# Chunk 1's softmax with tokens on partitions, a shorter weight conversion, and an identity made by VectorE

## The chip, the cores and the metric

The kernel runs on one core of one Trainium2 chip. The metric is the device time of one execution in microseconds (us). Before the change the median of three runs was 972.17 us (971.12 to 972.57).

## The reference

Pooled attention feeds a two-layer feed-forward net. Keys and values are averaged over groups of 8 positions, so each head of a batch has 72 pooled keys for 576 queries.

```python
def _attn_ref(q, k, v):                      # (8, 8, 576, 64) float32 each
    k_p = k.reshape(B, H, Sp, pool, D).mean(axis=3)
    v_p = v.reshape(B, H, Sp, pool, D).mean(axis=3)
    scores = scale * np.matmul(q, k_p.transpose(0, 1, 3, 2))
    scores = scores - np.max(scores, axis=-1, keepdims=True)
    attn = np.exp(scores)
    attn = attn / (np.sum(attn, axis=-1, keepdims=True) + 1e-09)
    return np.matmul(attn, v_p).astype(np.float32)

def _moe_ref(x, w_in, w_out):                # x (4608, 512); weights 512x2048 and 2048x512
    h = np.maximum(x @ w_in, 0.0)
    return (h * h @ w_out).astype(np.float32)
```

The two weight matrices arrive as 64-bit floats and are turned into 32-bit floats on the chip.

## The kernel before

**Chunks and steps.** The 4608 tokens are cut into 12 chunks of 384. Each chunk needs 16 steps, one for each 128 columns of the hidden layer. A step `(c, fc)` puts on TensorE the hidden product `h` of this step (line 480), then the pieces of attention that are due, then the output product `o` of two steps earlier (`project`, line 517, `LAG` = 2). ScalarE applies the ReLU and, in chunks 0 and 1, the square (`r`, lines 498 to 500). `h` has two PSUM buffers, so a new `h` waits until ScalarE has read the one before the last. Chunk 0 multiplies plain float32 (weights `wf`). Later chunks split every operand in a high and a low float32r part (`xh`, `xl`, `gh`, `gl`, `w`) and add three products.

**Attention.** It runs by pairs of heads, four pairs to a chunk: `transpose_q` (PSUM `qps`, copied to `st`), scores (`sps`), softmax, `weigh_values` (`av`, copied to `x`). Chunk 0 keeps tokens on partitions: `token_scores` (line 403) leaves 96 tokens by 4x72 keys, so that VectorE takes maxima and sums along the free axis (`tm`); `token_turn` (line 437) then turns the result with eight transposes (`pps`) and ScalarE copies it to `sc`. Chunk 1 and later keep the keys on partitions: `scores` (line 315) hands its copy to GpSimd, which reduces over partitions (`mx` for the maxima, `tot` for the sums), and the sums go through DRAM and back to become reciprocals (`rs`, `rc`, `rr`, `rd`, `rb`, lines 372 to 399).

**Weights.** Each of the 32 weight tiles (`raw`) is landed by a DMA. `magnitude` (ScalarE, one instruction) writes the absolute value of the high word to `wf`. `to_float32` (VectorE) then clips it, shifts and masks it, and ors in the sign bits and the top bits of the low word: four instructions, two keys at a time.

**What sets the order.** `InOrder` records each instruction in the order in which the program issues it, engine by engine, and an engine works it off in that order. Loads go out on SP's queue, in the order in which `load` was called before `issue_loads` (line 106). Before the steps comes a start that is written out by hand (lines 546 to 609): loads, pooling of batch 0's and batch 1's keys and values (chunk 1 holds tokens of both batches), and chunk 0's attention. Values are pooled on TensorE against a matrix of `ones` (`pool_v_pair`, PSUM `vps`). `keep_busy` multiplies the identity with itself. After that, a table `work` lists what is due at which step; `EARLY` gives the first step of each pair of chunk 1 and the offsets of its stages. The loop at the end (lines 653 to 674) reads it: first `h`, then what TensorE owes, then `project`, then the work of the other engines, the conversion, the loads, and ScalarE's `r` last.

```python
IDLE = (3, 1)
EARLY = ((-19, -16, -13, -10), (0, 2, 3, 5, 5, 6, 7, 8))
FIRST, EAGER, AHEAD = 2, 8, 5
```

PSUM pools: `ps_o` three banks (outputs, and chunk 0's scores), `ps_h` two, `ps_a` three (everything else).

Of the kernel before, what the change touches and what calls it, by code (L numbers as in the profile page):

```python
# [32 lines left out]
def pooled_attn_relu2_ffn(  # L33
# [281 lines left out]
    def scores(c, p):  # L315
# [3 lines left out]
        early = c == 1  # L319
        if early:  # L320

            blocks = st.rearrange("p (i t s) -> p i t s", i=2, s=QT)
            for i in range(2):
                h = 2 * p + i
                for t, (b, _, _) in enumerate(segments(c)):
                    for two in range(2):
                        rows = slice(two * D, (two + 1) * D)
                        PE.matmul(ss[two][:SP_, (i * 2 + t) * QT:(i * 2 + t + 1) * QT], lhsT=kf[b][rows, h // KH, h % KH * SP_:(h % KH + 1) * SP_],
                                  rhs=blocks[rows, i, t, :], start=True, stop=True)
        else:  # L330
            for i in range(2):
                h = 2 * p + i
                for b, o, n in segments(c):
                    kh, kl, _ = kv[b]
                    for j, kk in enumerate((kl, kh)):
                        PE.matmul(ss[i][:SP_, o:o + n], lhsT=kk[:, h * SP_:(h + 1) * SP_], rhs=st[:, i, o:o + n], start=j == 0, stop=j == 1)

        def then():
            if early:
                sc = w_tile(F32, f"sc_{c}_{p}")[:SP_, :, :CH]  # L340
                cols = sc.rearrange("p i (t s two) -> p two i t s", two=2, s=QT)
                for two in range(2):
                    ACT.copy(cols[:, two], ss[two][:SP_, :CH].rearrange("p (i t s) -> p i t s", i=2, s=QT))
            else:
                sc = sb.tile([SP_, 2, CH], F32, name=f"sc_{c}_{p}", tag="sc", bufs=SCB)
# [9 lines left out]
    def reduced(kind, c, p):  # L355
        names = [f"{kind}_{c}_{p}_{i}" for i in range(2)]
        if c == 1:
            return [half_tile("m", x)[:SP_, :CH] for x in names]
        return [sb.tile([SP_, CH], F32, name=x, tag="mx", bufs=3) for x in names]
# [345 lines left out]
```

## Time and profile before

| what | value |
|---|---|
| median of 3 runs | 972.17 us (971.12 to 972.57) |
| the profiled execution | 971.68 us, of which the span of its instructions 969.9 us |
| TensorE busy | 946.1 us, 98% |
| VectorE / ScalarE / GpSimd busy | 628.5 / 428.3 / 394.1 us |
| DMA | 64.45 MB, 66 GB/s over the span |

A line of the timeline gives start, duration, engine, operation, the tile written and the tiles read, shapes and the number of merged instructions; in brackets stands the idle time of the engine before it and what ended it. PEld is TensorE's weight load, SPq a DMA issued by SP. A float32 product with 128 or 96 columns shows as two records for each instruction, a transpose as one. Half tiles share a name: two keys, or two small tiles, show under the name of the first of them, so `wf_o` and `wf_i` both stand for converted weights of either matrix.

### The profile page before, as it was taken

How to read it: one execution, taken by the hardware profiler on the slowest of the kernel's cores; microseconds unless marked ns; L12 is line 12 of the kernel's file. 1: busy time of each engine (PE TensorE's matmuls, PEld its weight loads, DVE VectorE, ACT ScalarE, POOL GpSimd, SP SyncE). 2: the span in 40 equal slices, each digit the busy share in tenths (PEclk: the TensorE clock that was granted, in tenths of full speed). 3: DMA queues.
4: the chain of work that ended last, by engine and by line, in shares of the span. 5: the costliest groups of instructions: out<-in, count | busy, mean ns of one | idle time of the engine just before them, and what ended most of it. 6: DMA issues, size and time to landing. Idle time of an engine off the chain costs nothing.

```text
span 969.9 us, 13344 instructions
## 1 busy us (share of the span) xinstructions
PE 946.1 (98%) x4888; PEld 793.5 (82%) x4888; DVE 628.5 (65%) x1034; ACT 428.3 (44%) x847; POOL 394.1 (41%) x209
## 2 busy tenths in 40 slices
PE   5989899999999999999999999999999999999998
PEld 5644457888888888888888888888888888888997
DVE  4869997877765556767775656667776555453221
ACT  1644466774434445344444434443543434432322
POOL 4288733544344443443434335343534534440000
PEclk9999999999999999999999999999999999999999
DMA  9926212112211112112112102102311210100000
GB/s 239 365 95 217 82 34 66 48 52 87 60 45 62 38 38 70 34 51 92 54 39 76 37 20 78 52 30 52 95 52 30 77 32 18 58 10 9 33 1 32
DMA packets 53361, 64.45 MB, mean 66 GB/s; under 512 B 14936, under 2 KB 34480, under 8 KB 53296
## 3 DMA queue, kind: packets, MB, share of 16 engines
q1 hardware_dynamic: 53296, 63.61, 21.4%
q8 instruction: 38, 0.62, 0.3%
q14 instruction: 27, 0.22, 0.1%
HBM read 53.87 MB, written 9.71 MB: 66 GB/s over the span
## 4 chain that ended last, share of the span: by engine, by line
PE 85%; DVE 8%; issue 3%; DMA 2%; ACT 1%; POOL 0%; SPq 0%; DVEq 0%; POOLq 0%
PE o L29 38%; PE h L29 37%; PE av L29 4%; PE sps L29 3%; DVE wf_o L29 2%; DVE wf_i L29 2%; PE qps L29 1%; PE vps L29 1%; DMA q<-in_q_dram 1%; DMA rd<-rr 0%; DVE st L29 0%; PE kps L29 0%; DVE sc L29 0%; DVE kp L29 0%; POOL tot L29 0%
## 5 line engine op out<-in xcount | busy, mean ns | idle before, releaser
L29 PE MATMUL h<-xh,w_i 128*128 128x384 f32 x1408 | 389.1, 337 | 0.0
L29 POOL PARTITION_ALL_REDUCE tot<-sc x88 | 250.1, 2889 | 217.8 <-issue 201.6
L29 PE MATMUL o<-w_o,gh 128*128 128x512 f32 x1056 | 335.2, 398 | 0.4 <-ACT ob L29 0.4
L29 PEld LDWEIGHTS h<-xh,w_i 128*128 128x128 f32 x1408 | 258.7, 188 | 8.5 <-issue 0.5
L29 PE MATMUL h<-xl,w_i 128*128 128x384 f32 x704 | 238.0, 338 | 0.0
L29 PEld LDWEIGHTS o<-w_o,gh 128*128 128x128 f32 x1056 | 192.6, 188 | 52.1 <-issue 15.3
L29 POOL PARTITION_ALL_REDUCE mx<-sc x88 | 131.4, 1540 | 243.6 <-ACT sc L29 243.6
L29 DVE TENSOR_TENSOR gl<-r,gh 128x384 fp32r<-128x384 f32 x176 | 146.5, 832 | 108.4 <-ACT gh L29 106.5
L29 PE MATMUL o<-w_o,gl 128*128 128x512 f32 x528 | 208.7, 395 | 0.0
L29 DVE TENSOR_TENSOR r<-r 128x384 f32<-128x384 f32 x160 | 105.7, 661 | 108.7 <-ACT r L29 108.3
L29 ACT CAST gh<-r 128x384 fp32r<-128x384 f32 x176 | 90.4, 514 | 150.1 <-DVE r L29 149.6
L29 PEld LDWEIGHTS h<-xl,w_i 128*128 128x128 f32 x704 | 132.2, 188 | 8.1 <-issue 0.7
L29 ACT ACTIVATE r<-h 128x384 f32<-128x384 f32 x192 | 93.8, 488 | 99.9 <-PE h L29 98.6
L29 PEld LDWEIGHTS o<-w_o,gl 128*128 128x128 f32 x528 | 99.1, 188 | 22.5
L29 DVE TENSOR_TENSOR st<-qps,st 64x384 fp32r<-64x384 f32 x80 | 60.3, 754 | 48.1 <-ACT st L29 47.2
L29 ACT CAST st<-qps 64x384 fp32r<-64x384 f32 x80 | 59.4, 742 | 52.6 <-PE qps L29 52.0
L29 ACT ACTIVATE sc<-sc 72x384 f32<-72x384 f32 x88 | 43.7, 525 | 70.1 <-DVE sc L29 70.1
L29 ACT CAST xh<-rb 128x384 fp32r<-128x384 f32 x44 | 22.6, 513 | 108.5 <-DVE rb L29 108.5
L29 DVE TENSOR_REDUCE vp<-v 72x64 f32<-72x512 f32 x48 | 51.0, 1063 | 0.0
L29 DVE TENSOR_REDUCE kp<-k 96x64 f32<-96x512 f32 x42 | 43.7, 1041 | 3.4 <-DMA k<-in_k_dram 3.4
L29 DVE TENSOR_TENSOR sc<-sc,mx 72x384 f32<-72x384 f32 x88 | 44.6, 546 | 0.0
L29 PE MATMUL av<-sc,vp 72*64 72x384 f32 (+1 forms) x256 | 43.1, 425 | 0.9 <-ACT sc L29 0.9
(82 smaller groups left out, 701.8 us busy)
## 6 DMA issues: line engine op xcount, KB each, us to landing
k<-in_k_dram SPq DMA_DIRECT2D x48, 192.0 KB
out_dram<-ob SPq DMA_DIRECT2D x36, 256.0 KB
rb<-rd SPq DMA_DIRECT2D x88, 96.0 KB
raw_i<-in_moe_w_in_dram SPq DMA_DIRECT2D x16, 512.0 KB
raw_o<-in_moe_w_out_dram SPq DMA_DIRECT2D x16, 512.0 KB
v<-in_v_dram SPq DMA_DIRECT2D x48, 144.0 KB
q<-in_q_dram SPq DMA_DIRECT2D x30, 192.0 KB
q<-in_q_dram SPq DMA_DIRECT2D x32, 96.0 KB
```

What stands on the lines that cost most here:

```text
L29: return lambda *a, **k: self.tc.keep_in_program_order(f(*a, **k))
```

## The change

- The identity, which GpSimd made, is now made by VectorE (a ramp of indices, a transpose, four comparisons). `keep_busy` issues 16 and 2 products, not 3 and 1.
- `magnitude` scales the absolute value by 2^16, and a second ScalarE instruction writes the wanted top bits of the low word, as a whole number, over that word. `to_float32` then needs three VectorE instructions and not four.
- Chunk 1 uses `token_scores`, `token_normalise` and `token_turn` as chunk 0 does. Its exponentials read PSUM and take the negated maximum as bias, one instruction for each block of 72 keys. Its sums no longer go through DRAM, and GpSimd's reductions begin with chunk 2. `EARLY` has five stages and its first pair starts at step 0.
- Chunk 1's first query tile and two further weight tiles are loaded ahead of batch 1's values. Two of the four poolings of these values, and the transposes of batch 1's keys, move from the start into steps 0, 2 and 3. The copy of `vps` goes from VectorE to ScalarE.

```diff
-EXP_MIN = 2.0 ** -15
-EXP_MAX = 122879.9921875
+SHIFT = 2.0 ** 16
+EXP_MIN = 2.0 ** -15 * SHIFT
+EXP_MAX = 122879.9921875 * SHIFT
+LOW = 7.4999 / 65535
...
-    IDLE = (3, 1)
+    IDLE = (16, 2)
-    EARLY = ((-19, -16, -13, -10), (0, 2, 3, 5, 5, 6, 7, 8))
+    EARLY = ((-16, -13, -10, -7), (0, 1, 2, 3, 4))
...
-    make_identity(nc, ident)
+    ramp = const.tile([P, 2, 32], F32, name="ramp")
+    DVE.memset(ident, 0.0)
+    DVE.memset(ramp[:, 0, :1], 0.0)
+    for n in (1, 2, 4, 8, 16):
+        DVE.tensor_scalar(ramp[:, 0, n:2 * n], ramp[:, 0, :n], float(n), None, op0=ALU.add)
+    DVE.transpose(ramp[:, 1, :], ramp[:, 0, :])
+    for n in range(0, P, 32):
+        rows = slice(n, n + 32)
+        DVE.tensor_scalar(ident[rows, rows], ramp[rows, 0, :], ramp[rows, 1, :1], None, op0=ALU.is_equal)
...
-        ACT.activation(wf[key].rearrange("p (a n) -> p a n", a=2), words[..., 1].bitcast(F32), AF.Abs)
+        ACT.activation(wf[key].rearrange("p (a n) -> p a n", a=2), words[..., 1].bitcast(F32), AF.Abs, scale=SHIFT)
+        halves = raw[key].bitcast(U16).rearrange("p a (n w) -> p a n w", w=4)
+        ACT.activation(words[..., 0], halves[..., 1], AF.Copy, scale=LOW)
...
             DVE.tensor_scalar(m, m, EXP_MIN, EXP_MAX, op0=ALU.max, op1=ALU.min)
-        for _, _, m in parts:
-            DVE.tensor_scalar(m, m, 3, 0x3FFFFFF8, op0=ALU.logical_shift_left, op1=ALU.bitwise_and)
         for words, _, m in parts:
-            DVE.scalar_tensor_tensor(m, words[..., 1], 0xC0000000, m, op0=ALU.bitwise_and, op1=ALU.bitwise_or)
+            DVE.scalar_tensor_tensor(m, m, 3, words[..., 0], op0=ALU.logical_shift_left, op1=ALU.bitwise_or)
         for words, _, m in parts:
-            DVE.scalar_tensor_tensor(m, words[..., 0], 29, m, op0=ALU.logical_shift_right, op1=ALU.bitwise_or)
+            DVE.scalar_tensor_tensor(m, words[..., 1], 0x80000000, m, op0=ALU.bitwise_and, op1=ALU.bitwise_or)
...
-            DVE.tensor_copy(kv[b][2][:, 2 * p:2 * p + 2, :].rearrange("s h d -> s (h d)"), pt[:SP_, :2 * D])
+            ACT.copy(kv[b][2][:, 2 * p:2 * p + 2, :].rearrange("s h d -> s (h d)"), pt[:SP_, :2 * D])
...
+    def token_banks(c, p, name, tag):
+        if c:
+            return [ps_a.tile([P, 512], F32, name=f"{name}_{c}_{p}_{j}", tag="a") for j in range(2)]
...
             for i in range(2):
-                DVE.tensor_reduce(m[:, i, 0], views[i], axis=AX.X, op=ALU.max)
+                DVE.tensor_reduce(m[:, 0, i], views[i], axis=AX.X, op=ALU.max)
+                if c:
+                    DVE.tensor_scalar(m[:, 1, i], m[:, 0, i], -SCALE, None, op0=ALU.mult)
...
+                for t in range(NQ if c else 0):
+                    ACT.activation(e[i][:, t], views[i][:, t], AF.Exp, bias=m[:, 1, i, t:t + 1], scale=SCALE)
...
             xh, xl = xts[c]
+            if c == 1:
+                split(xh[:, p, :], xl[:, p, :], av[:, :CH])
+                return
...
-    for p in range(NPAIR):
-        load_v_pair(1, p)
+    load_q(1, 0)
...
-    for key in first_keys:
+    for key in keys[:FIRST + 2]:
         land(key)
-    for key in keys[FIRST:EAGER]:
+    for p in range(NPAIR):
+        load_v_pair(1, p)
+    for key in keys[FIRST + 2:EAGER]:
         land(key)
...
-        after = [token_scores(0, p + 2)] if p + 2 < NPAIR else []
-        after.append(pool_v_pair(1, p))
+        after = [token_scores(0, p + 2), pool_v_pair(1, p)] if p + 2 < NPAIR else []
...
     for hf in range(2):
-        transpose_k(1, hf)()
+        at(0, transpose_k, 1, hf)
         at(9 + hf, split_k, 1, hf)
+    for p in range(2, NPAIR):
+        at(p, pool_v_pair, 1, p)
...
+        names = (transpose_q, token_scores, token_normalise, token_turn, weigh_values) if c == 1 else stages
```

TensorE's order between the start and step 1, by pairs of heads: the first number after a tile's name is the batch or chunk, the next the pair. Before:

```order
L29 MATMUL vps_1_2_396<-vv_1_2_98,ones_80 72x128 x6
L29 MATMUL av_0_1_403<-sc_0_1_378,vp_0_154 64x384 x2
L29 MATMUL pps_0_2_0_410<-ident_75,te_0_2_332 72x96 x4
L29 MATMUL pps_0_2_1_411<-ident_75,te_0_2_332 72x96 x4
L29 MATMUL vps_1_3_430<-vv_1_3_99,ones_80 72x128 x6
L29 MATMUL av_0_2_437<-sc_0_2_420,vp_0_154 64x384 x2
L29 MATMUL pps_0_3_0_441<-ident_75,te_0_3_382 72x96 x4
L29 MATMUL pps_0_3_1_442<-ident_75,te_0_3_382 72x96 x4
L29 MATMUL av_0_3_463<-sc_0_3_451,vp_0_154 64x384 x2
L29 MATMUL kps_1_0_468<-ident_75,kp_1_0_266 128x96 x3
L29 MATMUL kps_1_1_473<-ident_75,kp_1_3_279 128x96 x3
L29 MATMUL qps_1_0_484<-ident_75,q_1_0_478 128x96 x4
```

The same place after the change:

```order
L34 MATMUL av_0_1_423<-sc_0_1_405,vp_0_182 64x384 x2
L34 MATMUL pps_0_2_0_432<-ident_75,te_0_2_359 72x96 x4
L34 MATMUL pps_0_2_1_433<-ident_75,te_0_2_359 72x96 x4
L34 MATMUL av_0_2_451<-sc_0_2_442,vp_0_182 64x384 x2
L34 MATMUL pps_0_3_0_455<-ident_75,te_0_3_409 72x96 x4
L34 MATMUL pps_0_3_1_456<-ident_75,te_0_3_409 72x96 x4
L34 MATMUL av_0_3_474<-sc_0_3_465,vp_0_182 64x384 x2
L34 MATMUL h_0_0_509<-x_0_390,wf_i_0_0_427 128x384 x4
L34 MATMUL kps_1_0_515<-ident_75,kp_1_0_293 128x96 x3
L34 MATMUL kps_1_1_519<-ident_75,kp_1_3_306 128x96 x3
L34 MATMUL qps_1_0_523<-ident_75,q_1_0_105 128x96 x4
L34 MATMUL h_0_1_550<-x_0_390,wf_i_0_0_427 128x384 x4
```

Two value poolings are gone from this place, and the first `h` now stands ahead of the transposes of batch 1's keys. The two other poolings keep theirs: the first stands right ahead of chunk 0's first `pps`, here after the change.

```order
L34 MATMUL sps_0_2_0_325<-kf_0_183,st_0_2_283 96x72
L34 MATMUL sps_0_2_1_326<-kf_0_183,st_0_2_283 96x72
L34 MATMUL vps_1_0_338<-vv_1_0_110,ones_89 72x128 x6
L34 MATMUL pps_0_0_0_345<-ident_75,te_0_0_222 72x96 x4
L34 MATMUL pps_0_0_1_346<-ident_75,te_0_0_222 72x96 x4
```

ScalarE's order after the change, from the third weight tile after the last copy of chunk 0's `x` to the first ReLU:

```order
L34 ACTIVATE wf_i_1_2_491<-raw_i_1_2_114 128x512
L34 ACTIVATE raw_i_1_2_114<-raw_i_1_2_114 128x512
L34 ACTIVATE wf_i_1_2_491<-raw_o_1_115 128x512
L34 ACTIVATE raw_o_1_115<-raw_o_1_115 128x512
L34 COPY kf_1_514<-kps_1_0_515 128x288
L34 COPY kf_1_514<-kps_1_1_519 128x288
L34 COPY st_1_0_530<-qps_1_0_523 128x384
L34 ACTIVATE wf_o_2_532<-raw_o_2_116 128x512
L34 ACTIVATE raw_o_2_116<-raw_o_2_116 128x512
L34 ACTIVATE wf_o_2_532<-raw_i_2_0_117 128x512
L34 ACTIVATE raw_i_2_0_117<-raw_i_2_0_117 128x512
L34 ACTIVATE r_0_0_547<-h_0_0_509 128x384
```

Each weight tile has two rows here where it had one. With the two tiles ahead of these rows, twelve such rows, for six tiles, stand between that copy and the first ReLU.

More of the change, by code (lines that the diff above doesn't have):

```diff
@@ L7 @@
 from concourse import mybir
-from concourse.masks import make_identity
 from concourse._compat import with_exitstack
@@ L13 @@
 U32 = mybir.dt.uint32
+U16 = mybir.dt.uint16
 AF = mybir.ActivationFunctionType
@@ L318, in scores @@
         ss = [ps_a.tile([P, 512], F32, name=f"sps_{c}_{p}_{i}", tag="a") for i in range(2)]
[L319 to L336, printed above, removed]
-        def then():
[L339 to L345, printed above, removed]
+        for i in range(2):
+            h = 2 * p + i
+            for b, o, n in segments(c):
+                kh, kl, _ = kv[b]
+                for j, kk in enumerate((kl, kh)):
+                    PE.matmul(ss[i][:SP_, o:o + n], lhsT=kk[:, h * SP_:(h + 1) * SP_], rhs=st[:, i, o:o + n], start=j == 0, stop=j == 1)
+        def then():
+            sc = sb.tile([SP_, 2, CH], F32, name=f"sc_{c}_{p}", tag="sc", bufs=SCB)
             mx = reduced("mx", c, p)
             for i in range(2):
-                if not early:
-                    ACT.copy(sc[:, i, :], ss[i][:SP_, :CH])
+                ACT.copy(sc[:, i, :], ss[i][:SP_, :CH])
                 GP.partition_all_reduce(mx[i], sc[:, i, :], channels=SP_, reduce_op=bass_isa.ReduceOp.max)
@@ L355, in reduced @@
     def reduced(kind, c, p):
[L356 to L359, printed above, removed]
+        return [sb.tile([SP_, CH], F32, name=f"{kind}_{c}_{p}_{i}", tag="mx", bufs=3) for i in range(2)]
     def exponents(c, p):
@@ L430, in token_normalise @@
         for i in range(2):
-            DVE.tensor_reduce(m[:, i, 1], e[i], axis=AX.X, op=ALU.add)
-        DVE.tensor_scalar(m[:, :, 2], m[:, :, 1], 1e-9, float(POOL), op0=ALU.add, op1=ALU.mult)
-        DVE.reciprocal(m[:, :, 3], m[:, :, 2])
+            DVE.tensor_reduce(m[:, 2, i], e[i], axis=AX.X, op=ALU.add)
+        DVE.tensor_scalar(m[:, 3], m[:, 2], 1e-9, float(POOL), op0=ALU.add, op1=ALU.mult)
+        DVE.reciprocal(m[:, 3], m[:, 3])
         for i in range(2):
-            DVE.tensor_tensor(e[i], e[i], m[:, i, 3].unsqueeze(2).to_broadcast([QT, NQ, SP_]), op=ALU.mult)
+            DVE.tensor_tensor(e[i], e[i], m[:, 3, i].unsqueeze(2).to_broadcast([QT, NQ, SP_]), op=ALU.mult)
     def token_turn(c, p):
         e, _ = live.pop((c, p))
-        pt = [ps_h.tile([P, 512], F32, name=f"pps_{c}_{p}_{i}", tag="h") for i in range(2)]
+        pt = token_banks(c, p, "pps", "h")
         for i in range(2):
@@ L445, in then @@
             sc = sb.tile([SP_, 2, CH], F32, name=f"sc_{c}_{p}", tag="sc", bufs=SCB)
+            order = "p (s t two) -> p two t s" if len(segments(c)) == 1 else "p (t s two) -> p two t s"
             for i in range(2):
-                ACT.copy(sc[:, i].rearrange("p (s t two) -> p two t s", t=NQ // 2, two=2),
+                ACT.copy(sc[:, i].rearrange(order, t=NQ // 2, two=2),
                          pt[i][:SP_, :CH].rearrange("p (two t s) -> p two t s", t=NQ // 2, two=2))
@@ L571, in pooled_attn_relu2_ffn @@
     keep_busy(IDLE[0])
-    for i in range(KT + 1):
+    for i in range(KT + 2):
         pool_k(0, i)
     transpose_k(0, 0)()
-    pool_k(0, KT + 1)
     transpose_q(0, 0)()
@@ L645, in pooled_attn_relu2_ffn @@
             s = c * NFC + first[p]
-            at(s - QL, load_q, c, p)
-            for d, f in zip(offsets, stages):
+            if c > 1 or p:
+                at(s - QL, load_q, c, p)
+            for d, f in zip(offsets, names):
                 at(s + d, f, c, p)
     last = (to_float32, split_weights)
-    on_pe = (transpose_q, transpose_k, scores, token_scores, token_turn, weigh_values)
+    on_pe = (transpose_k, transpose_q, scores, token_scores, token_turn, weigh_values, pool_v_pair)
     for s in range(-PRO, len(steps) + LAG):
```

19 lines of the change are left out of this document (12 added, 7 removed).

## The prediction

> **What bounds the kernel now.** On the page TensorE is busy for 98% of the span, so I looked for the other 2%: first the busy time by stage, then TensorE's waits, then the timeline around them. The stages:
>
> ```profile
> 44.00:100.00 56.00, 51.24 (x199) 26.66 (x200) 46.92 (x88) 29.98 (x61) 49.33 (x12) 1.00 0.49 161
> 100.00:153.00 53.00, 50.47 (x178) 28.39 (x176) 50.01 (x82) 26.41 (x53) 25.88 (x12) 1.00 0.20 60
> 153.00:960.00 807.00, 805.92 (x4225) 707.69 (x4224) 503.21 (x795) 351.35 (x698) 305.91 (x154) 1.00 0.16 47
> ```
>
> A row gives the stretch and its length, then busy time of TensorE, weight loads, VectorE, ScalarE, GpSimd, then clock, DMA share and GB/s. After 153 us TensorE rests 1 us in 807, and nothing that the change touches lies there. So what counts is when that part begins. Two pieces precede it: the start, up to the first `h` at 43.8, and chunk 0's steps, in which VectorE is busy 97 us of 109. TensorE's waits in those steps:
>
> ```profile
> PE h L29 <- ACT r L29: 3.3, 2, 2.1
> PE h L29 <- DVE wf_i L29: 3.2, 4, 1.2
> PE sps L29 <- DVE st L29: 0.7, 1, 0.7
> ```
>
> Together 7.2 us in seven waits. The timeline shows where they come from:
>
> ```profile
> 45.02 3.32 POOL L29 PARTITION_ALL_REDUCE mx<-sc  x2 [17.27 <-ACT sc L29]
> 50.81 1.56 PE L29 MATMUL h<-x,wf_o 128*128 128x384 f32 x4 [1.19 <-ACT r L29]
> 53.03 1.56 PE L29 MATMUL h<-x,wf_i 128*128 128x384 f32 x4 [0.66 <-DVE wf_i L29]
> 54.52 0.88 PE L29 MATMUL sps<-st,kf 64*72 64x96 f32 x16
> ...
> 88.26 12.28 POOL L29 PARTITION_ALL_REDUCE tot<-sc  x2 [2.60 <-issue]
> 91.68 1.42 DVE L29 TENSOR_SCALAR wf_o<-wf_o 128x512 f32<-128x512 f32 x4
> 93.03 0.68 DVE L29 SCALAR_TENSOR_TENSOR wf_o<-raw_o,wf_o 128x512 uint32<-128x512 uint32 x1
> 97.00 1.45 PE L29 MATMUL h<-x,wf_o 128*128 128x384 f32 x4
> 97.38 4.39 DVE L29 TENSOR_SCALAR wf_i<-wf_i 128x512 f32<-128x512 f32 x4
> 98.29 1.45 PE L29 MATMUL h<-x,wf_i 128*128 128x384 f32 x4
> 99.58 2.74 PE L29 MATMUL o<-wf_i,r 128*128 128x512 f32 x6
> 102.15 1.45 PE L29 MATMUL h<-x,wf_o 128*128 128x384 f32 x4
> ```
>
> GpSimd's two maxima (45.02, 3.3 us) hold back the exponentials, in front of which ScalarE's ReLU cannot pass: `h` waits at 50.81 for a PSUM buffer. And four VectorE scalings that mostly take 1.42 us take 4.39 at 97.38, where GpSimd's sums (88.26, 12.3 us) end, so the converted weights are late. Both mechanisms go with the change.
>
> **Chunk 0's steps after the change.** *Removed:* the seven waits, 7.2 us, and what a restart costs. The waiting `h` at 53.03 begins 1.49 us before the next group, an unhindered one 1.29 (97.00 to 98.29), so 0.2 each: 8.6 in all. *Added on TensorE:* per pair eight transposes like chunk 0's `pps`, and two poolings, three transposes twice, one `qps` and one `sps` that stood before the first `h`.
>
> ```profile
> 25.45 1.53 PE L29 MATMUL vps<-vv,ones 96*72 96x128 f32 x12
> 26.82 0.82 PE L29 MATMUL pps<-ident,te 96*72 96x96 f32 x8
> ...
> 41.26 0.71 PE L29 MATMUL kps<-ident,kp 96*128 96x96 f32 x6
> 43.02 0.88 PE L29 MATMUL sps<-st,kf 64*72 64x96 f32 x16 [0.57 <-ACT st L29]
> 43.83 2.85 PE L29 MATMUL h<-x,wf_i 128*128 128x384 f32 x8
> ```
>
> Start to start, a pooling takes 1.37 us (25.45 to 26.82), the batch-1 key and query transposes and the scores 2.0 (41.26 to 43.83 less the wait of 0.57). Four `pps` at 0.7 (0.82 less the drain of the last) make 2.8, two poolings 2.7. Added: 7.5. The scores themselves keep their count and size. *Can the other engines follow?* A step is 5.15 us of `h` and `o` (97.00 to 102.15: one `h` of eight records, six of `o`), plus a third of a pair, about 6. VectorE's conversion of two keys falls from 4.1 (1.42 and four of 0.68) to 3.4, and the softmax of a pair, by chunk 0's, is some 4 every third step: 4.7 in 6. ScalarE gains one instruction for each key, below: its 56.4 us in 109 become some 75. So TensorE sets the pace, once it is running.
>
> *A new wait at its beginning.* ScalarE has the twelve weight rows, two `kf` and one `st` ahead of the first ReLU. The second instruction of a key is not in the trace. Its nearest rows:
>
> ```profile
> 27.35 1.53 ACT L29 COPY sc<-pps 72x384 f32<-72x384 f32 x2 [2.40 <-PE pps L29]
> 28.20 0.87 PE L29 MATMUL sps<-kf,st 64*96 64x72 f32 x14 [0.24 <-DVE te L29]
> 31.39 0.48 ACT L29 COPY x<-av 128x384 f32<-128x384 f32 x1 [1.94 <-PE av L29]
> 34.69 1.26 ACT L29 ACTIVATE wf_i<-raw_i 128x512 f32<-128x512 f32 x2
> 41.37 0.48 ACT L29 COPY x<-av 128x384 f32<-128x384 f32 x1 [0.95 <-PE av L29]
> 41.77 0.70 ACT L29 COPY kf<-kps 128x288 f32<-128x288 f32 x2
> ```
>
> The magnitude of a key, with the same strides, takes 0.6 (34.69, two in 1.26); that is what I take. Bounds are 0.35 (a 288-wide plain copy, 41.77) and 0.77 (a scattered copy, 27.35). Then the ReLU ends 6.9 + 0.7 + 0.5 + 0.5 = 8.6 us after the last copy of `x`. TensorE in that time does two `h` (5.2) and batch 1's 1.5 to 2.0, and stands 1.7 before the third `h`. The eight exponentials of 72 keys are bounded by 0.1 each (0.35 for 288 columns, 0.48 for 384, carried down) and 0.35; at 0.2 a pair costs ScalarE 1.6, inside its slack of 34 us. Sum of this piece: 7.5 - 8.6 + 1.7 = +0.6.
>
> **The start after the change.** The identity came from GpSimd at 9.4. From VectorE it should come near 3 us: twelve small instructions at about 0.2, like the reciprocal at 25.00. Everything up to chunk 0's third pair of scores moves up, by 4 to 6 us. But then TensorE's next instruction is the pooling of batch 1's first values (order above), and these now land behind a query tile and four weight tiles:
>
> ```profile
> 9.41 1.65 PE L29 MATMUL idle<-ident 128*128 128x128 f32 x6 [9.41 <-POOL ident masks.py:199]
> 16.09 1.25 POOL L29 TENSOR_TENSOR k<-k 96x256 f32<-96x256 f32 x2 [5.01 <-DMA k<-in_k_dram]
> 25.00 0.20 DVE L29 RECIPROCAL tm<-tm 96x8 f32<-96x8 f32 x1
> ...
> 20.00:25.00 5.00, 4.39 (x50) 3.90 (x48) 3.32 (x11) 1.67 (x4) 4.53 (x11) 1.00 1.10 271
> 25.00:30.00 5.00, 4.76 (x59) 4.36 (x56) 4.75 (x13) 2.10 (x4) 2.59 (x6) 1.00 1.03 388
> ...
> k<-in_k_dram SPq DMA_DIRECT2D x48, 192.0 KB
> raw_i<-in_moe_w_in_dram SPq DMA_DIRECT2D x16, 512.0 KB
> vv<-in_v_dram SPq DMA_DIRECT2D x8, 288.0 KB
> ```
>
> The DMA engines are full (share 1.03 to 1.10), so bytes are time. Batch 1's first key tile arrives at 16.09. Behind it now come five key tiles and a query tile of 192 KB each, four weight tiles of 512 KB and 288 KB of values: 1.47 MB at 271 GB/s and 2.10 MB at 388, 5.4 + 5.4, so 27.0. (All at 388 would give 25.3, all at 271 29.3.) The same pooling began at 25.45 before, so the gain of the identity is spent waiting: TensorE rests some 6 us. From there the chain is as before, `pps`, `sc`, `av`, `x`, pair by pair on ScalarE: 5.7 to the first copy of `x` (25.45 to 31.39 before, less the wait of 0.24 for VectorE at 28.20), 9.98 to the last (31.39 to 41.37), plus 1.2 for two more weight instructions ahead of the third pair, plus the copy's 0.48. The copies of `vps` (0.28 on VectorE) fit in ScalarE's idle 1.94 and 0.4; uncovered they would add 0.5. The first `h` starts at 27.0 + 5.7 + 10.0 + 1.2 + 0.5 = 44.4 and not 43.83: +0.6.
>
> **Sum.** +0.6 + 0.6 = +1.2 us: span 971.1, execution 972.9 (971.68 - 969.9 = 1.8 lies outside the span), and, since the profiled execution lies 0.5 below the median, **973.4 us** for the median. Its own bounds: landing -1.7 to +2.3, second weight instruction -2.0 to +1.4 (eight of them count), waits that stay 0 to 2; so 970 to 978.
>
> **Rivals.** *TensorE slows down in its rest* (slower, 0.25). The trace has two paces:
>
> ```profile
> 11.33 1.49 PE L29 MATMUL qps<-ident,k 96*128 96x96 f32 x8
> 15.26 4.27 PE L29 MATMUL vps<-vv,ones 96*72 96x128 f32 x24
> 23.56 0.82 PE L29 MATMUL qps<-ident,q 96*128 96x96 f32 x8
> ```
>
> The same eight transposes take 1.49 and 0.82, though the granted clock reads 1.00: TensorE ran at about half pace at first. It still did at 15.26 (24 records of pooling in 4.27, 0.18 each) and no longer at 25.45 (12 in 1.53). Afterwards its longest wait is 2.1 us, so no row shows whether a rest of 6 takes the pace away again. [...] If so, pooling, `pps`, `sps` and pooling (1.37 + 0.8 + 0.8 + 1.37 = 4.3) take 1.8 times as long, +3.5, and products further down the chain up to 3 more; with 1 for the first `h`, +4 to +7: about 977.5 us. [...]
>
> *The values arrive in time* (faster, 0.27). If value tiles land beside the weights and not behind them, or the chain after them is shorter than before because VectorE is idle, `pps` of the first pair starts near 22 and the last `x` comes 5 us sooner: 968 us. For it: VectorE loses its `vps` copies and its fourth conversion step. Against: the order of the loads, and ScalarE's extra work in the same place.
>
> *ScalarE's second weight instruction is dear* (slower, 0.10): at 1.0 us, beyond the bound, +0.8 in the start and +2.4 before the third `h`: 976 us.
>
> **Chances.** Forecast 0.38, the three rivals 0.25, 0.27 and 0.10. A measurement here can tell 0.2%, 1.9 us, from no change. The faster case and 0.06 of the forecast give 0.33 for faster; 0.26 of the forecast alone lies within; the rest is slower, 0.41. The range, 966.5 to 978.5, reaches into the faster case and takes in the slow pace.
>
> **What would show it.** Right: GpSimd idle from its key pooling to step 11; no wait of `h` on `r` or `wf` after the third `h`; a wait of `vps` on `vv` of about 6 us, ending near 27; the first `h` near 44.4; first `r` 8 to 9 us after. Wrong: a first `h` before 41 or after 46, eight `pps` in 1.5 us after the rest (the slow pace), or ScalarE's second weight instruction far from 0.6.

## The result, and the profile after

The changed kernel takes 980.99 us (median; 980.81 to 982.25) where the kernel before, on the same chip, took 972.37: a ratio of 1.010, interval 1.0068 to 1.0131. It is slower by 1.0%, and above the forecast's range (966.5 to 978.5). All four executions agree, with a mean granted clock of 0.983 or 0.984. The profiled one took 982.25 us, its span 980.5; before it was 971.68 and 969.9.

First the busy time by stretches, in the same columns as before (the third number from the end is the granted clock of TensorE):

```profile
24.00:25.00 1.00, 0.00 (x0) 0.00 (x0) 0.96 (x4) 0.00 (x0) 0.92 (x3) 0.95 1.13 301
25.00:51.00 26.00, 20.60 (x88) 13.04 (x88) 10.41 (x26) 11.05 (x21) 3.12 (x7) 0.50 1.05 349
51.00:55.00 4.00, 4.00 (x7) 2.19 (x7) 2.04 (x5) 3.79 (x8) 0.00 (x0) 0.50 1.04 293
55.00:57.00 2.00, 2.00 (x14) 1.46 (x13) 2.00 (x6) 1.73 (x5) 0.00 (x0) 0.84 0.38 100
57.00:117.00 60.00, 58.71 (x281) 34.05 (x279) 41.91 (x95) 44.37 (x108) 0.00 (x0) 1.00 0.34 109
117.00:121.00 4.00, 4.00 (x9) 1.70 (x6) 2.16 (x3) 3.96 (x8) 0.00 (x0) 0.57 0.00 2
```

The clock falls to half at 24.9 (0.95 over that microsecond: a tenth of it at half), stays there through the rest of chunk 0's attention, and returns near 55.6. It falls once more from 117.0 to 120.5. In the kernel before this column reads 1.00 throughout. The timeline of TensorE shows what that does:

```profile
3.37 5.95 PE L34 MATMUL idle<-ident 128*128 128x128 f32 x32 [3.37 <-DVE ident L34]
12.36 2.81 PE L34 MATMUL vps<-vv,ones 96*72 96x128 f32 x24 [0.43 <-DMA vv<-in_v_dram]
27.68 2.80 PE L34 MATMUL vps<-vv,ones 96*72 96x128 f32 x12 [5.36 <-DMA vv<-in_v_dram]
30.28 1.49 PE L34 MATMUL pps<-ident,te 96*72 96x96 f32 x8
44.96 2.23 PE L34 MATMUL av<-sc,vp 72*64 72x384 f32 x4 [2.10 <-ACT sc L34]
51.10 5.07 PE L34 MATMUL h<-x,wf_i 128*128 128x384 f32 x8
56.84 2.77 PE L34 MATMUL h<-x,wf_i 128*128 128x384 f32 x8
116.42 0.96 PE L34 MATMUL av<-sc,vp 72*64 72x192 f32 x8 [1.29 <-ACT te L34]
117.31 4.40 PE L34 MATMUL o<-wf_o,r 128*128 128x512 f32 x6
150.36 0.74 PE L34 MATMUL h<-xh,w_i 128*128 128x384 f32 x1
```

The identity is ready at 3.37 (9.41 before), and TensorE has its full pace by 12.36, where 24 pooling records take 2.81 us. Then it rests 5.36 us for batch 1's values. After the rest twelve pooling records take 2.80 (1.53 before), eight `pps` 1.49 (0.82), and eight records of the first `h` 5.07 (2.85). The first `h` starts at 51.10 and not at 43.83. At 116.42 there is a wait of 1.29 that the kernel before did not have, and the six `o` behind it take 4.40 and not 2.74.

The span grew by 10.6 us: 7.3 until the first `h`, 3.1 from there to chunk 1's first `h` (51.10 to 150.36, where it was 43.83 to 140.02), 0.3 in everything after.

ScalarE and the waits of the steps (the last two rows: waits of TensorE from 35 to 155 us, by sum, count and longest):

```profile
41.85 0.66 ACT L34 ACTIVATE wf_i<-raw_i 128x512 f32<-128x512 f32 x1
42.41 0.66 ACT L34 ACTIVATE raw_i<-raw_i 128x512 uint32<-128x512 uint16 x1
51.21 0.48 ACT L34 COPY x<-av 128x384 f32<-128x384 f32 x1 [1.63 <-PE av L34]
59.69 0.50 ACT L34 ACTIVATE r<-h 128x384 f32<-128x384 f32 x1
125.28 3.77 POOL L34 PARTITION_ALL_REDUCE mx<-sc  x2 [96.92 <-ACT sc L34]
...
PE av L34 <- ACT sc L34: 2.7, 3, 2.1
PE av L34 <- ACT te L34: 1.3, 1, 1.3
```

The second instruction for a key costs what the first does, 0.66 as recorded and 0.56 from start to start. GpSimd is idle for 96.92 us, until 125.28. None of the seven waits of the kernel before is left: the change removed what the prediction said it would.

### The profile page after: what moved, and what is told of

It reads as the page before. It is cut to its first block, busy times and chain, and to the rows that moved or that the text cites. A ratio compares the mean times of both kernels' runs of the same rounds, so it can differ in the third digit from the quotient of the medians.

```text
span 980.5 us, 13461 instructions
## 1 busy us (share of the span) xinstructions
PE 961.5 (98%) x4948; PEld 807.2 (82%) x4948; DVE 612.4 (62%) x1026; ACT 450.2 (46%) x911; POOL 333.4 (34%) x191
## 4 chain that ended last, share of the span: by engine, by line
PE 96%; DMA 2%; ACT 1%; SPq 1%; issue 0%; DVE 0%; ACTq 0%
PE o L34 43%; PE h L34 42%; PE av L34 4%; PE sps L34 3%; PE qps L34 1%; DMA vv<-in_v_dram 1%; PE vps L34 1%; DMA k<-in_k_dram 1%; PE pps L34 1%; DMA k<-in_q_dram 1%; SPq L34 1%; PE kps L34 0%; ACT sc L34 0%; ACT raw_i L34 0%; ACT wf_i L34 0%
## 5 line engine op out<-in xcount | busy, mean ns | idle before, releaser
L34 POOL PARTITION_ALL_REDUCE tot<-sc x80 | 201.2, 2562 | 208.6 <-issue 198.6
L34 POOL PARTITION_ALL_REDUCE mx<-sc x80 | 119.2, 1538 | 322.9 <-ACT sc L34 322.9
L34 ACT CAST xh<-rb 128x384 fp32r<-128x384 f32 x40 | 20.5, 513 | 95.2 <-DVE rb L34 95.2
L34 ACT ACTIVATE sc<-sc 72x384 f32<-72x384 f32 x80 | 39.8, 525 | 46.0 <-DVE sc L34 46.0
L34 DVE TENSOR_REDUCE vp<-v 72x64 f32<-72x512 f32 x48 | 50.9, 1061 | 0.0
L34 PE MATMUL av<-sc,vp 72*64 72x384 f32 (+1 forms) x256 | 46.5, 448 | 4.0 <-ACT sc L34 2.7
L34 DVE TENSOR_TENSOR sc<-sc,mx 72x384 f32<-72x384 f32 x80 | 40.6, 547 | 0.0
```

Source lines behind the costliest of these rows:

```text
L34: return lambda *a, **k: self.tc.keep_in_program_order(f(*a, **k))
```

## The experiments

The theory after this reading: TensorE's clock is lost where TensorE is only sparsely busy, and the change made the start sparse in two ways, by a rest for the values that now land late and by taking two poolings out of the gaps of the chain behind. The rival: the late landing and the added work cost the time by themselves. Each kernel is given with its median and its ratio to the kernel before on the same chip, whose median was 970.0 to 971.2 in the four groups of runs. Idle products are products of the identity with itself, whose result nobody reads.

### Idle products in the rest: `fill20`, `fill10`

```diff
-        after = [token_scores(0, p + 2), pool_v_pair(1, p)] if p + 2 < NPAIR else []
+        after = [token_scores(0, p + 2)] if p + 2 < NPAIR else []
+        if p == 0:
+            keep_busy(20)          # fill10: 10
+        if p + 2 < NPAIR:
+            after.append(pool_v_pair(1, p))
```

> The changed kernel with twenty idle products of the identity put in TensorE's queue right ahead of batch 1's first value pooling, where TensorE rests 5.36 us after the change. They move no data and change no order. Theory (the rest takes the pace away): the granted clock stays at 1.00 through 27 to 51 us, twelve pooling records take 1.5 us and not 2.80, the first h starts near 44.4 and its eight records take 2.9 us and not 5.07: about 6.7 + 2.2 = 9 us less, some 972 us. Rival (the late landing of the values and the work added to the start and the steps cost the time by themselves): within 1 us of the changed kernel, 980 to 982. If the clock accounts for half, 976.

> As the run with twenty idle products, with ten: they end near 24.8, so that a rest of some 2.8 us remains before the pooling. In the changed kernel the clock fell 2.6 us after the last product. If a rest of that length is short enough to keep the pace: 972 us, as with twenty. If the pace goes within such a rest: 979 to 981. The rival that puts the cost on the late landing: 980 to 982.

`fill20`: 977.18 (974.95 to 980.29), ratio 1.007 (1.005 to 1.009). `fill10`: 981.82 (977.19 to 985.04), ratio 1.011 (1.008 to 1.015). The first gained 3.8 us of the 9 that the theory gave; the second nothing clear. The timeline of `fill20`, and one microsecond of its stretches:

```profile
28.02 1.50 PE L34 MATMUL vps<-vv,ones 96*72 96x128 f32 x12 [1.27 <-DMA vv<-in_v_dram]
39.73 2.25 PE L34 MATMUL av<-sc,vp 72*64 72x384 f32 x4 [2.75 <-ACT sc L34]
45.89 4.50 PE L34 MATMUL h<-x,wf_i 128*128 128x384 f32 x8
...
39.00:40.00 1.00, 0.27 (x1) 0.27 (x2) 1.00 (x3) 1.00 (x2) 0.00 (x0) 0.51 1.02 389
```

The rest is filled and the pooling takes 1.50, at full pace. But the clock falls later, at 39.0, in a wait of 2.75 for ScalarE: one of the two poolings that the change moved away stood there, and ScalarE has two more weight instructions. In `fill10` the values landed later and left a rest of 4.40 us, not 2.8. The pooling and the microsecond ahead of it:

```profile
29.34 2.81 PE L34 MATMUL vps<-vv,ones 96*72 96x128 f32 x12 [4.40 <-DMA vv<-in_v_dram]
...
28.00:29.00 1.00, 0.00 (x0) 0.00 (x0) 0.00 (x0) 0.00 (x0) 0.63 (x3) 0.89 1.10 246
```

The clock fell at 28.8, nearly 4 us into the rest, so this profile does not tell what a rest of 2.8 does.

### One part of the change undone: `values_first`, `pool_later`, `pool_back`

`values_first` loads batch 1's values ahead of the query tile and the weights, as before. `pool_later` keeps the late landing and moves the remaining two poolings into the steps. `pool_back` is `values_first` with all four poolings in the start.

```diff
+    for p in range(NPAIR):             # values_first, pool_back
+        load_v_pair(1, p)
     load_q(1, 0)
...
-    for p in range(NPAIR):
-        load_v_pair(1, p)
...
-        after = [token_scores(0, p + 2), pool_v_pair(1, p)] if p + 2 < NPAIR else []
+        after = [token_scores(0, p + 2)] if p + 2 < NPAIR else []
+        after.append(pool_v_pair(1, p))       # pool_back alone
...
-    for p in range(2, NPAIR):
+    for p in range(NPAIR):                    # pool_later alone; pool_back: none
         at(p, pool_v_pair, 1, p)
```

> The changed kernel with the order of the loads alone undone: batch 1's four value tiles again ahead of the query tile and of all weight tiles. Theory (the rest takes the pace away): the values land near 22 to 23, TensorE has no rest above 2.5 us, the clock stays at 1.00, the first h starts at 39 to 41 and the time is 967 to 970, below the kernel before. Rival (the clock is harmless, the landing costs): the first h comes 5 us sooner than after the change, near 46, 975 to 976. Rival (the added work in the start and the steps costs): 979 or more.

> The changed kernel with all four poolings of batch 1's values in the steps (two were left in the start), so that nothing in the start waits for these values. TensorE then waits only for VectorE's first normalised pair, near 24.5. Theory (the rest takes the pace away): a rest of some 2 us, clock 1.00, first h near 40, and 2.7 us more work in the steps: 968 to 971. If a rest of 2 us takes the pace away too: first h near 46, 976 to 978. Rival (added work costs): 979 or more.

> The changed kernel with two parts undone: batch 1's values are loaded ahead of the weights again, and all four poolings of these values stand in the start again, between the products that wait for ScalarE, as before. Theory (the clock falls where TensorE is sparsely busy for some 3 us, and the poolings filled the gaps): the mean granted clock is 0.995 or more in every run, with no run like the two at 977 to 978 of the kernel that undoes the loads alone; first h near 40, no pooling left in the steps (2.7 us), 964 to 967 us. Rival (only a long rest takes the pace away, the poolings are just work that has to stand somewhere): same as with the loads alone, 969, bimodal again.

| kernel | median (range), us | ratio to before (interval) | first `h` in the profile | mean clock of the executions |
|---|---|---|---|---|
| `values_first` | 969.43 (968.86 to 978.13) | 0.9997 (0.9968 to 1.0026) | 46.06 | 0.991 to 0.995 in eight, 0.983 in two |
| `pool_later` | 972.72 (972.07 to 974.18) | 1.0026 (1.0011 to 1.0041) | 39.11 | 0.986 to 0.991 |
| `pool_back` | 966.74 (965.63 to 969.14) | 0.9952 (0.9934 to 0.9971) | 39.79 | 0.993 to 0.996 |

`values_first` is the clearest. One and the same kernel takes 968.9 to 971.3 where its mean clock was 0.991 to 0.995, and 977.4 and 978.1 where it was 0.983. The median is within the theory's 967 to 970, but its clock of 1.00 came in no execution. The profiled execution is one of the latter two. Its longest wait of TensorE ahead of the fall, and its stretches:

```profile
17.86 1.53 PE L34 MATMUL vps<-vv,ones 96*72 96x128 f32 x12 [1.04 <-ACT vp L34]
...
19.00:20.00 1.00, 0.72 (x8) 0.54 (x6) 0.75 (x2) 0.24 (x1) 0.98 (x3) 1.00 1.08 277
20.00:21.00 1.00, 0.71 (x4) 0.61 (x4) 0.00 (x0) 0.24 (x1) 0.92 (x2) 0.61 1.10 280
```

The clock fell at 20.2 without any long rest: after TensorE's first product the longest before it was 1.04. So my first wording, that the rest takes the pace, was too narrow. The "some 3 us" of the next theory is an estimate: the clock had fallen 2.6 us into the rest of the changed kernel, 3.8 into that of `fill10` and 2.0 into the wait of `fill20`. `pool_later` misses its 968 to 971 a little: the clock falls at 28.3 and is back at 41.9. With the poolings back in the gaps the kernel is faster than before, within the 964 to 967 expected (its clock, expected at 0.995 or more, was 0.993 in one execution); its profiled execution still lost the clock from 35.2 to 42.1.

### The same loss in the kernel before: `before_sparse`

```diff
-        after.append(pool_v_pair(1, p))
+        if p < 2:
+            after.append(pool_v_pair(1, p))
...
+    for p in range(2, NPAIR):
+        at(p, pool_v_pair, 1, p)
```

> The kernel before with one thing of the change: the third and fourth pooling of batch 1's values move from the start into steps 2 and 3. Nothing rests for a load. Theory (the poolings kept TensorE busy enough in the chain of the start): the clock, 0.998 to 1.00 in every run of the kernel before, falls to 0.5 near 36 to 42 us in most runs, mean 0.990 to 0.996, time 973 to 976. Rival (only a rest of several us takes the clock away): clock 0.998 or more, and the chain is as long or shorter, 969 to 971.

973.43 (970.90 to 976.78), ratio 1.0028 (1.0004 to 1.0052). The mean clock is 0.992 to 0.994 in all ten executions. The kernel before, of 24 executions beside it, had 0.995 in one and 0.998 or more in the others. Stretches, and the first `h`:

```profile
34.00:36.00 2.00, 0.76 (x8) 0.48 (x6) 1.90 (x8) 2.00 (x5) 0.00 (x0) 0.89 1.16 278
36.00:38.00 2.00, 1.80 (x4) 0.58 (x4) 2.00 (x7) 0.86 (x2) 0.00 (x0) 0.50 1.12 275
...
46.29 4.28 PE L29 MATMUL h<-x,wf_i 128*128 128x384 f32 x8
```

Nothing lands later here and no work is added; two poolings stand elsewhere, and the clock falls at 35.6, where they had been. The first `h` comes later, not earlier, and slower (4.28, not 2.85). This rules out, for this part, that late landing or added work is needed for the loss. The clock does not explain the times of this kernel among themselves, though: the four executions at 0.994 took 976.0 to 976.8, the six at 0.992 or 0.993 only 970.9 to 973.7.

### Everything kept as in the change, gaps filled: `fill_all`

The change with the twenty idle products of `fill20` and, in addition:

```diff
+        if p > 1:
+            keep_chain((3, 11)[p - 2], f"idle_c{p}")   # idle products into a free PSUM bank
         if p:
             weigh_values(0, p - 1)()
...
+    keep_chain(7, "idle_c4")
     weigh_values(0, NPAIR - 1)()
```

> The changed kernel with idle products alone: the twenty ahead of the first value pooling as in fill20, and 3, 11 and 7 more ahead of the last three av of the start, where TensorE waits for ScalarE (2.75 us at the third in fill20, whose clock fell to 0.5 at 39.0). No transfer and no order is changed. Theory (sparse work takes the clock): clock 1.00 through the start, the first h at 43 to 44 and not 45.89, at full pace: 971 to 973 us, 4 to 6 below fill20. Rival (fill20's rest of the loss is the added work): 976 to 977.

978.03 (973.79 to 986.83), ratio 1.0074 (1.0045 to 1.0104): a miss by 5 us. The profiled execution (979.60) shows why:

```profile
29.04 2.71 PE L34 MATMUL vps<-vv,ones 96*72 96x128 f32 x12 [2.09 <-DMA vv<-in_v_dram]
47.19 2.85 PE L34 MATMUL h<-x,wf_i 128*128 128x384 f32 x8
56.02 2.53 PE L34 MATMUL h<-x,wf_o 128*128 128x384 f32 x4 [1.71 <-ACT r L34]
```

The fillers of the chain work: the first `h` has its full pace, 2.85. But the values came later (the pooling began at 27.68, 28.02, 29.34 and 29.04 in the four profiles that have this order of loads and this pooling in the start), and at the end of a rest of 2.09 the clock fell for 3.4 us (29.2 to 32.6). Then the third `h` waits 1.71 for ScalarE, and it fell again (56.5 to 59.9). The one execution whose mean clock was 1.00 took 973.79 us. That is what the change with these idle products takes when the clock is kept.

### The collision at step 10: `pool_back_q2`

`pool_back` with:

```diff
-                at(s - QL, load_q, c, p)
+                at(s - QL - (2 if (c, p) == (2, 0) else 0), load_q, c, p)
             for d, f in zip(offsets, names):
-                at(s + d, f, c, p)
+                at(s + d - (2 if (c, p, d) == (2, 0, 0) else 0), f, c, p)
```

> As pool_back, and chunk 2's first query tile is loaded and transposed two steps earlier (step 8 and not 10). After the change av of chunk 1's third pair waits 1.29 us at step 10, behind two banks of scores and one of these transposes in a pool of three banks; in the changed kernel's profile the clock then falls to 0.50 from 117.0 to 120.7 as well. If that collision is the cause: the wait goes, and with it 1.3 us, and 3 where the clock fell: 1.3 to 3 us below pool_back. If the wait is ScalarE's lateness: it moves elsewhere, and the time is as pool_back's.

965.13 (964.33 to 966.55), ratio 0.9943 (0.9921 to 0.9965): 1.6 us below `pool_back`, as forecast, though the two ranges overlap. The timelines are clearer. From the second `h` to chunk 1's first `pool_back` took 91.64 us, with a wait and a second loss of the clock (103.5 to 106.9), and `pool_back_q2` 88.45 (first three rows `pool_back`, last two `pool_back_q2`):

```profile
44.41 2.77 PE L34 MATMUL h<-x,wf_i 128*128 128x384 f32 x8
102.05 0.87 PE L34 MATMUL av<-sc,vp 72*64 72x192 f32 x8 [1.29 <-ACT te L34]
136.05 0.74 PE L34 MATMUL h<-xh,w_i 128*128 128x384 f32 x1
...
44.80 2.77 PE L34 MATMUL h<-x,wf_i 128*128 128x384 f32 x8
133.25 0.74 PE L34 MATMUL h<-xh,w_i 128*128 128x384 f32 x1
```

The wait of 1.29 is gone without a successor. It came from the pool of three PSUM banks: two for the scores of chunk 1's last pair, one for chunk 2's first query transposes, none for `av` until the exponentials have read a score bank. Behind the same 1.29 the clock fell in six profiles (the changed kernel, `values_first`, `pool_later`, `pool_back`, `fill_all`, `softmax_only`) and not in two (`fill20`, `fill10`).

### Each part of the change alone: `ident_only`, `convert_only`, `softmax_only`

`ident_only` and `convert_only` are the kernel before with VectorE's identity and `IDLE = (16, 2)`, or with the three-instruction conversion. `softmax_only` is the change with these two, the order of the loads, the four poolings and the `vps` copies as before. Its edit, without the code of the softmax itself, which is that of the change:

```diff
 # softmax_only, against the kernel before
-    EARLY = ((-19, -16, -13, -10), (0, 2, 3, 5, 5, 6, 7, 8))
+    EARLY = ((-16, -13, -10, -7), (0, 1, 2, 3, 4))
...
+        names = (transpose_q, token_scores, token_normalise, token_turn, weigh_values) if c == 1 else stages
...
-        transpose_k(1, hf)()
+        at(0, transpose_k, 1, hf)
```

> The kernel before with one part of the change: VectorE makes the identity, and 16 and 2 idle products follow it. In the start no load order and no pooling is changed. The kernel that undoes the loads alone began its first batch-1 pooling at 22.6 where the kernel before began at 25.45. Theory (the identity is worth what the start gains, and a start that stays dense keeps its clock): first h near 41, clock 0.998 or more, some 3 us below the kernel before. Rival (the chain of the start waits for something else, VectorE or a load): first h at 43 to 44, within 1 us of the kernel before.

> The kernel before with the conversion of the change alone: two ScalarE instructions and three VectorE instructions for a key in place of one and four. By the prediction's terms: the waits for converted weights, 3.2 us and 4 restarts of 0.2, go or shrink; ScalarE's two further instructions delay the first h by 1.2, and six more a third h by up to 1.7: from -2.8 to +1 against the kernel before, with the clock kept. If the longer wait of the third av takes the clock (0.996 or less): 1 to 3 us slower.

> The change without its identity, its conversion, its order of the loads, its move of two poolings and its vps copies on ScalarE: chunk 1's softmax with tokens on partitions is left, with the transposes of batch 1's keys and the first query tile in step 0 and its query tile loaded in the start. By the prediction's terms: 8.6 us of waits go (GpSimd has no sums or maxima until chunk 2), 2.8 are added for four pps, and 1.3 for the wait at step 10 (3.1 if the clock falls there): 2.7 to 4.5 us below the kernel before. Rival (VectorE's conversion stays late without GpSimd): the waits for weights stay, 3 us less gained: 0 to 2 below.

| kernel | median (range), us | ratio (interval) | mean clock |
|---|---|---|---|
| `ident_only` | 967.55 (967.15 to 978.01) | 0.9994 (0.9955 to 1.0033) | 0.996 to 1.00 in seven, 0.982 to 0.984 in three |
| `convert_only` | 968.02 (963.37 to 973.11) | 0.9975 (0.9946 to 1.0005) | 0.998 in two, 0.993 or 0.994 in eight |
| `softmax_only` | 970.63 (965.28 to 972.38) | 0.9982 (0.9957 to 1.0007) | 0.998 to 1.00 |

None is clear by time alone. With the clock kept `ident_only` takes 967.2 to 968.0; the three executions that lost it took 977.6 to 978.0. `convert_only` takes 963.4 and 963.6 with the clock at 0.998, 6.5 below the kernel before and more than the 2.8 expected. Of its other eight executions four are 1.6 to 3.0 slower than the kernel before, as expected, and four 1.8 to 3.9 faster. `softmax_only` misses its 2.7 to 4.5 by the median; its two executions at 1.00 took 965.3 and 965.9. The parts are better sized in the timelines, between the first or second `h` of chunk 0 and the first of chunk 1. Of `convert_only`, with its waits of `h` in the steps, and of `softmax_only`:

```profile
55.99 2.77 PE L35 MATMUL h<-x,wf_i 128*128 128x384 f32 x8
141.53 0.74 PE L35 MATMUL h<-xh,w_i 128*128 128x384 f32 x1
...
PE h L35 <- ACT r L35: 1.4, 1, 1.4
```

```profile
44.10 2.85 PE L30 MATMUL h<-x,wf_i 128*128 128x384 f32 x8
105.50 0.87 PE L30 MATMUL av<-sc,vp 72*64 72x192 f32 x8 [1.29 <-ACT te L30]
139.49 0.74 PE L30 MATMUL h<-xh,w_i 128*128 128x384 f32 x1
```

The conversion alone takes the piece from the second `h` from 93.17 us (46.85 to 140.02 before) to 85.54. It removes the waits for weights and, beyond what I expected, those for `r` too, but for one of 1.4. The softmax alone takes the piece from the first `h` from 96.19 to 95.39; the prediction's terms give 96.19 - 8.6 + 2.8, plus 2.0 for batch 1's work, which here stands behind the first `h`, 1.3 and 0.2 for the wait at step 10, and 1.7 for the clock lost at 106.3 to 109.7: 95.6.

### The start made dense: `best`, `dense_front`, `dense_all`

All three are `pool_back_q2` with idle products. `best`: six and three ahead of the last two `av` of the start. `dense_front`: five and three in the earlier rests of 1.04 and 0.57, at 17 to 21 us. `dense_all`: both.

```diff
-    after = [pool_v_pair(0, 2), pool_v_pair(0, 3)]
+    after = [pool_v_pair(0, 2)]
+    keep_busy(5)
+    after.append(pool_v_pair(0, 3))
     transpose_q(0, 2)()
+    keep_busy(3)
     transpose_q(0, 3)()
...
+        if p == 3:
+            keep_chain(6, "idle_c3")
...
+    keep_chain(3, "idle_c4")
     weigh_values(0, NPAIR - 1)()
```

> pool_back_q2 (the change with the loads and the poolings as before and chunk 2's first query tile two steps earlier), with six and three idle products ahead of the last two av of the start, where its clock still fell to 0.5 from 37 to 43 us behind a wait of 1.49. Theory (sparse work takes the clock): clock 0.998 or more, the fourth av takes 1.56 and not 2.22, the first h's eight records 2.9 and not 4.84: 2 to 3 us below pool_back_q2, 962 to 963. What can take it back: with h at full pace the third h waits for ScalarE, up to 1.7 (1.71 in fill_all).

> pool_back_q2 with five and three idle products in the earlier rests of the start: ahead of the fourth value pooling of batch 0 (rest 1.04 us, near 17.5) and of the fourth query transposes (0.57, near 20). In three kernels with the early identity the clock fell near 20 to 24 in 2 or 3 of 10 runs, at 8 to 10 us (values_first 977 to 978 against 969, ident_only 978 against 967.5, best 973 to 976 against 964). Theory (any sparse stretch of some 3 us can take the clock, by where it lies in time): no run of this kernel loses it there, all within 964 to 967. Rival (the early fall has another cause, the loads or the chip): again 2 or 3 of 10 runs 8 to 10 us above the rest.

> As dense_front, with the six and three idle products of best ahead of the last two av as well: the whole start dense. Theory: all runs at 963.5 to 965, clock 0.997 or more, without the three runs at 973 to 976 that best had. Rival: again some runs 9 us above.

| kernel | median (range), us | ratio (interval) | mean clock |
|---|---|---|---|
| `best` | 964.45 (963.73 to 975.77) | 0.9967 (0.9934 to 1.0001) | 0.997 to 1.00 in seven, 0.986 to 0.989 in three (972.9 to 975.8) |
| `dense_front` | 964.85 (964.31 to 965.71) | 0.9932 (0.9908 to 0.9957) | 0.994 to 0.997 |
| `dense_all` | 964.30 (963.52 to 964.90) | 0.9930 (0.9906 to 0.9953) | 0.998 to 1.00 |

`best` misses its 962 to 963: seven executions took 963.7 to 965.8; of the three others the profiled one lost the clock early, from 24.0 to 44.4. The two dense kernels are within what was expected. `dense_all` is faster than both kernels of the case, by 0.7% against the one before. Its timeline, its one wait in the steps, and its stretches:

```profile
38.76 2.85 PE L34 MATMUL h<-x,wf_i 128*128 128x384 f32 x8
47.57 1.56 PE L34 MATMUL h<-x,wf_o 128*128 128x384 f32 x4 [1.69 <-ACT r L34]
132.29 0.74 PE L34 MATMUL h<-xh,w_i 128*128 128x384 f32 x1
...
PE h L34 <- ACT r L34: 1.7, 1, 1.7
...
20.00:40.00 20.00, 19.97 (x167) 14.89 (x165) 13.25 (x34) 13.81 (x30) 7.38 (x16) 1.00 1.05 370
40.00:60.00 20.00, 18.31 (x83) 10.64 (x83) 18.48 (x40) 19.88 (x44) 0.00 (x0) 1.00 1.06 337
```

TensorE is busy 19.97 of 20 us in the start and the clock never falls. That buys only 0.5 us over `dense_front`, which is not clear of noise: with the first `h` at full pace the third waits 1.69 for ScalarE's ReLU, which stands behind the weights.

Whether the idle products at 17 to 21 us prevent the early fall is not settled, nor does any run show that its place in time decides. Outside a long rest only two profiles have it, `values_first` at 20.2 and `best` at 24.0; for the rest I go by the mean clock. By that it did not come in the twelve executions of the two dense kernels (0.994 to 1.00), and came in three of ten of `best` (0.986 to 0.989) and of `ident_only` (0.982 to 0.984); but `pool_back` and `pool_back_q2`, which have the same rests, did not show it in thirteen (0.993 to 0.996).

## Why the prediction was wrong

**The bound: right.** Only the start and chunk 0's steps counted; from chunk 1's first `h` on, the span differs by 0.3 us.

**Chunk 0's steps: right, in their terms.** The 8.6 of waits went: in the changed kernel no `h` waits at all. For the converted weights either part is enough. In `softmax_only`, where GpSimd is idle from 28 to 114.42, no `h` waits for them; in the kernel before VectorE's four scalings took 4.39 at 79.34 and 97.38. `convert_only` keeps the reductions, has fewer instructions, and loses these waits too. The second weight instruction takes 0.56 from start to start (0.6 forecast). The wait before the third `h`, forecast at 1.7, is 1.69 in `dense_all` and 1.71 in `fill_all`. The changed kernel does not show it, because its first `h` ran at half pace and gave ScalarE time; the first ReLU follows the last copy of `x` by 8.5 us (51.21 to 59.69), where 8.6 was worked out. From the first `h` to chunk 1's, `dense_all` takes 93.53 us; with the two poolings that it keeps out of there (2.7) that is 96.2, or 0 against before, where I had +0.6.

**The start up to the rest: right.** Identity at 3.37 (3), values at 27.68 (27.0), rest 5.36 (6). That the landing fits within 0.7 is in part luck: it was the earliest of four, which reach 29.34.

**The step that failed:** "From there the chain is as before", with 17.4 us from the pooling to the first `h`. It took 23.4, since TensorE had lost its pace (clock 0.50 from 24.9, 2.6 us into the rest of 5.36); in `fill20`, which kept the clock until 39.0, it took 17.9 (28.02 to 45.89). I had seen the two paces, 1.49 and 0.82 us for the same eight transposes, and gave the slow one 0.25 as a rival, against 0.38 for a forecast that needed the pace to survive. The row that spoke for survival, a longest wait of 2.1 in the kernel before, was a wait in the dense steps. It said nothing of 5 us in the sparse start.

**The rival's price was too low, too.** It had +4 to +7, about 977.5. Two of its terms, the up to 3 down the chain and the 1 for the first `h`, were my estimates, and no run shows them as they stand; what the runs showed in their place is below. The difference between the forecast span (971.1) and the measured (980.5) is made of: landing +0.7; the chain +6.0, inside what the rival had for it (3.5 and up to 3); the first `h` +2.2, where it had 1 (5.74 us to the second, 3.51 in `dense_all`); the wait at step 10, which I had not seen, +1.3 with 0.2 for its restart; the clock lost behind it +1.7 (six `o` in 4.40 for 2.74); the third `h`'s wait, which did not come, -1.7; and -1.0 that is left over in the steps. Sum +9.4. The forecast's own bounds, added up, give 969.7 to 979.1 and not 970 to 978; the measured time lies outside either.

I had stopped the rival where the chain ended. In the changed kernel the clock came back only 4.5 us into the first `h` (55.6), and a wait of 1.29 us was enough to be followed by a second loss (117.1 to 120.5).

**Rival "the values arrive in time": its gain exists, and needs an edit.** Ahead of the weights they allow the first `h` at 39 to 40 (`pool_back`, `ident_only`); the change's own order of loads spends it.

**What remains open.** The change with its clock kept throughout was seen in one execution only, 973.79 us, which agrees with the forecast of 973.4 and does not prove it. Why the values land anywhere from 27.7 to 29.3 with one order of loads was not tried, nor what made the clock fall at 20.2 us in the profile of `values_first` and at 24.0 in that of `best`, while most executions of both had a mean clock of 0.991 or more. Nor is it known why the kernel before spreads from 968 to 976 us in nearly all executions, with a mean clock of 0.995 or more. The slow pace at the beginning, which the clock's column does not show (last section), would fit, but only one execution of each kernel has a profile.

## What to carry to other kernels

Before an edit takes work out of TensorE's queue in a stretch where it waits for other engines, add up what is left there: the work that is moved may be what keeps the clock. In `before_sparse` the clock fell for 13.7 us where two poolings had stood; in the changed kernel the loss lasted 30.7. When a rival mechanism is priced, follow it to where it ends, not to where the stage ends, and look for the next short wait that may start it again (1.29 us here). Judge such a kernel by the mean clock of many executions beside their times: one profile can be of either kind, and the mean clock does not show all of the slow pace (the kernel before has 1.00, with 1.49 us for eight transposes at 11.33 and 0.82 at 23.56).
